# An mLSTM and two feed-forward layers on one core: the first layer's products in two row halves of the array

## The chip, the cores and the metric

The kernel runs on one core of a Trainium2 chip. The time is that of one execution on the device, in microseconds (us); the lower the better. Five engines work side by side, each through its own queue in order: PE (the matrix array, with its weight loads shown as PEld), DVE, ACT, POOL, and SP, which here only issues DMAs. An engine waits for another one, or for a DMA, at a semaphore.

## The reference

The inputs are q, k, v and an output gate of shape 2 x 8 x 768 x 40 (batch, head, position, head dimension), an input and a forget gate per position, and the weights of two feed-forward layers. All is float32.

```python
for t in range(S):                                # 768 positions
    m_new  = maximum(f[t] + m, i[t])
    f_stab, i_stab, m = exp(f[t] + m - m_new), exp(i[t] - m_new), m_new
    C = f_stab * C + i_stab * outer(v[t], k[t])   # 40 x 40 per head
    n = f_stab * n + i_stab * k[t]
    y[t] = sigmoid(o[t]) * (C @ q[t]) / maximum(abs(n . q[t]), 1)
x  = y as 1536 tokens x 320
xn = x / rms(x) * rms_g
x  = (silu(xn @ w_gate) * (xn @ w_val)) @ w_out   # first layer,  320 -> 1536 -> 320
h  = x @ w_in                                     # second layer, 320 -> 2048 -> 320
out = (maximum(h, 0) + alpha * minimum(h, 0)) @ w_out2
```

## The kernel before

**Stages.** The 768 positions are cut into six chunks of 128, and a chunk of one batch is a unit: units 0 to 11, of 128 tokens each. `attend` works out a unit: scores `sc` (L450), the part from the state `pv.../b` (L473), the weighted sum `pv` (L505), the new state `stp` (L529), then gate, division and scaling on ACT, DVE and POOL, and a transpose `trxn` (L627) that writes the unit's columns of `xh` and `xl`. The first layer takes groups m = 0, 1, 2 of 512 tokens (four units each). The second layer does the same with t2 = 0, 1, 2; its inputs go through a scratch tensor in memory and are transposed in 64-row halves (L657).

**Products in two parts.** Each float32 operand is split into a high part (a copy on ACT, fp32r) and a low part (what is left of it, from DVE or POOL). A product is high x high, high x low and low x high.

**First layer.** `moe1_in` (from L841) makes, for 128 hidden columns j of 512 tokens, two sums in a PSUM bank each: g from the gate's weights and v from the value's. `gemm_in` (L812) contracts over 320 rows in slabs of 128, 128 and 64. The third slab of the input stands twice, in rows 0 to 63 and again in rows 64 to 127, and the third slab of the weights has the high part of the gate's in the upper half and its low part in the lower one (for the value's the other way round), so that one matmul of 128 rows gives high and low together. That makes 8 matmuls of 512 columns for g and then 8 for v. After them come tanh (ACT, L856), silu (DVE, L859), the product with v (DVE, L862), the high part (ACT, L832) and the low part (DVE or POOL, L835). There are 36 such units of work: 12 for each m. For m = 0 the first four hold two j of 256 tokens each (32 matmuls of 256 columns), since only two units of tokens are there yet; the other 32 are wide (16 matmuls of 512 columns). `moe1_out` (L871) multiplies each result into four sums `acc` of 128 tokens, with three matmuls of 320 columns each (L826).

**Second layer.** `moe2_in` (from L933) has been working with 64 rows at a time: two sums h in two banks, and two matmuls side by side, one in rows 0 to 63 and one in rows 64 to 127 (L915). In phase 0 the upper rows write the first bank and the lower rows the second, 16 matmuls; in phase 1 the other way round, 14 matmuls. Between the phases stands `again` (L920): an ACT copy of one column of the input onto itself, which waits for phase 0 and on which phase 1 waits, so that no two halves write to a bank at once. `moe2_out` does the same with pairs of its four sums `accm` (L992, two runs of six matmuls, `again`, and two more runs with the banks changed).

**Order.** `plan` only notes steps, with the engine, a cost and the keys they read and write. `emit` (L79) then issues them in the order of the table `ORDER` (L1128), a list of step numbers; a trailing g puts a step on POOL that may run on DVE or POOL, and `*n` issues n idle matmuls on PE (`hot`, L1122; each shows as two in the profile). Each engine takes its steps in that order and waits where an input or one of the eight PSUM banks is not free.

**Names in the weights' preparation.** Weights come as raw words in blocks (`raw166w` and so on, from L695) and are decoded on ACT (L709, L715, L734), DVE (L719, L724) and DVE or POOL (L730, L738) before a product can use them.

## Time and profile before

| | us |
|---|---|
| median of three runs | 491.33 |
| their lowest and highest | 485.49, 492.27 |
| the profiled execution's own time | 490.37 |
| its span, first to last instruction | 488.6 |
| PE busy in the span | 463.8 (95%) |
| DVE, ACT, POOL busy | 321.6, 214.0, 154.3 |

Busy time counts the instructions of an engine from start to end, overlaps once. What lies between the span and the execution's own time is 490.37 - 488.6 = 1.8 us. The mean granted clock of the array over the span is 0.955 of the full 2.4 GHz; in a slice it is either near 1.00 or near 0.50 (1.2 GHz), or a mix of both.

### The profile page before, as it was taken

To read this page: it belongs to the slowest core of one execution; us is meant where nothing else is said; L and a number is where in the kernel's file an instruction comes from. 1 tells how busy PE (TensorE), PEld (TensorE's weight loads), DVE (VectorE), ACT (ScalarE), POOL (GpSimd) and SP (SyncE) were. 2 spreads that over 40 slices of the span, in tenths; PEclk is the share of its full clock that TensorE was granted. 3 is DMA by queue.
4 is the path that set the end of the run, shared out by engine and by line. 5 is a ranking of instruction groups with operands and counts; after the bars stand their busy time and mean duration, and the time that the engine had idled before them with its cause. 6 is when DMAs were issued, how large, how long until landed. Compare 5 with 4: busy or idle time off the path is not lost. (4 is left out here: it accounts for less than half of the span.)

```text
span 488.6 us, 9677 instructions
## 1 busy us (share of the span) xinstructions
PE 463.8 (95%) x3836; PEld 412.4 (84%) x3836; DVE 321.6 (66%) x592; ACT 214.0 (44%) x513; POOL 154.3 (32%) x156
## 2 busy tenths in 40 slices
PE   6988799989989999999998999999999999999996
PEld 5978798878869898888886888899989899888986
DVE  4669969889885554555487476598576475555354
ACT  3465674695543622533455534454523232222222
POOL 1242555687433203404156322221431101111310
PEclk9557799999999999999998999999999999999999
DMA  5657465455550311250134343063001010010001
GB/s 182 214 185 236 130 214 149 186 175 144 185 171 34 111 46 57 71 186 7 34 119 139 102 120 110 31 219 118 20 1 31 15 44 1 2 52 4 2 1 55
DMA packets 19149, 47.68 MB, mean 98 GB/s; under 512 B 2448, under 2 KB 8736, under 8 KB 19104
## 3 DMA queue, kind: packets, MB, share of 16 engines
q1 hardware_dynamic: 19104, 47.07, 30.2%
q8 instruction: 30, 0.49, 0.4%
q14 instruction: 15, 0.12, 0.1%
HBM read 40.07 MB, written 4.37 MB: 91 GB/s over the span
## 5 line engine op out<-in xcount | busy, mean ns | idle before, releaser
L962 DVE TENSOR_SCALAR tm<-hm,al_sb 128x512 f32<-128x512 f32 x48 | 35.3, 746 | 38.3 <-PE hm L915 27.0
L835 POOL TENSOR_TENSOR glm<-tm,ghm 128x512 fp32r<-128x512 f32 x17 | 21.9, 1293 | 110.2 <-ACT ghm L832 94.1
L832 ACT ACTIVATE ghm<-tm 128x512 fp32r<-128x512 f32 x48 | 29.8, 625 | 31.8 <-PE accm L992 16.7
L856 ACT ACTIVATE t<-g 128x512 f32<-128x512 f32 x36 | 21.3, 591 | 45.4 <-PE g L820 25.0
L835 DVE TENSOR_TENSOR glm<-tm,ghm 128x512 fp32r<-128x512 f32 x31 | 22.7, 737 | 27.2 <-ACT ghm L832 25.0
L859 DVE SCALAR_TENSOR_TENSOR t<-t,g 128x512 f32<-128x512 f32 x36 | 24.5, 682 | 24.4 <-ACT t L856 24.2
L835 POOL TENSOR_TENSOR gl<-t,gh 128x512 fp32r<-128x512 f32 x21 | 28.3, 1353 | 33.4 <-ACT gh L832 33.4
L832 ACT ACTIVATE gh<-t 128x512 fp32r<-128x512 f32 x36 | 22.4, 628 | 32.6 <-PE acc L826 16.5
L968 DVE SCALAR_TENSOR_TENSOR tm<-hm,tm 128x512 f32<-128x512 f32 x48 | 32.3, 686 | 0.8
L862 DVE SCALAR_TENSOR_TENSOR t<-t,v 128x512 f32<-128x512 f32 x36 | 24.4, 682 | 12.4 <-PE v L820 11.3
L505 PEld LDWEIGHTS pv<-vko,w 128*128 128x128 f32 x192 | 27.5, 220 | 4.6 <-DVE hn L482 3.0
L922 ACT ACTIVATE ghm<-ghm 128x1 fp32r<-128x1 f32 x48 | 9.6, 201 | 49.5 <-PE accm L992 49.3
L505 PE MATMUL pv<-vko,w 128*128 128x41 f32 x192 | 27.5, 303 | 3.6 <-DVE hn L482 2.3
L363 ACT ACTIVATE w<-w,col 128x128 f32<-128x128 f32 x80 | 26.5, 389 | 1.1 <-DVE col L297 0.8
L450 PE MATMUL sc<-r 40*128 40x128 f32 x192 | 18.5, 333 | 2.7 <-DVE xl L637 2.7
L450 PEld LDWEIGHTS sc<-r 40*128 40x128 f32 x192 | 15.6, 231 | 5.4 <-DVE xl L637 3.0
L574 POOL TENSOR_TENSOR vko<-vko,rd 128x320 f32<-128x320 f32 x7 | 6.9, 991 | 41.6 <-DVE rd L564 35.3
L454 DVE TENSOR_TENSOR w<-sc,w 128x512 f32<-128x512 f32 x24 | 16.0, 682 | 4.0 <-PE sc L450 3.1
L355 POOL TENSOR_SCALAR_AFFINE_SELECT w<-w 128x512 f32<-128x512 f32 x20 | 15.9, 812 | 8.0 <-ACT dec L370 7.9
L922 ACT ACTIVATE x2h<-x2h 128x1 fp32r<-128x1 f32 x24 | 4.8, 198 | 28.1 <-PE hm L915 28.1
L992 PE MATMUL accm<-o20h,ghm 64*128 64x320 f32 x96 | 16.8, 315 | 0.0
L992 PE MATMUL accm<-o20l,ghm 64*128 64x320 f32 x96 | 16.4, 306 | 0.0
(590 smaller groups left out, 1579.7 us busy)
## 6 DMA issues: line engine op xcount, KB each, us to landing
vko<-in_vko SPq DMA_DIRECT2D x12, 484.5 KB
w<-a_scr SPq DMA_DIRECT2D x10, 512.0 KB
r<-in_qk SPq DMA_DIRECT2D x24, 160.0 KB
y_scr<-y SPq DMA_DIRECT2D x12, 192.0 KB
x<-y_scr SPq DMA_DIRECT2D x12, 192.0 KB
out<-y SPq DMA_DIRECT2D x12, 160.0 KB
raw210w<-in_wo SPq DMA_DIRECT2D x1, 640.0 KB
raw218w<-in_wo SPq DMA_DIRECT2D x1, 640.0 KB
```

Of the source, the lines that this page charges most:

```text
L363: nc.scalar.activation(out=T[w][:, h], in_=T[w][:, h], func=AF.Exp, bias=T[f"col{c}"][:, g:g + 1])
L450: nc.tensor.matmul(T[f"sc{u}_{s}"][:, i], lhsT=q[:, 1, i], rhs=q[:, 0, i], start=True, stop=True)
L454: nc.vector.tensor_tensor(out=p, in0=T[f"sc{u}_{s}"], in1=p, op=ALU.mult)
L505: nc.tensor.matmul(ps[:, i, 0:V1], lhsT=T[w][:, h], rhs=v[:, h], start=True, stop=True)
L832: nc.scalar.activation(out=new(gh, "gh", [128, n], F32R), in_=T[t], func=AF.Copy)
L835: on[e].tensor_tensor(out=new(gl, "gl", [128, n], F32R), in0=T[t], in1=T[gh].bitcast(F32), op=ALU.subtract)
L856: nc.scalar.activation(out=new(t, "t", [128, 512]), in_=T[g], func=AF.Tanh, scale=0.5)
L859: nc.vector.scalar_tensor_tensor(out=T[t], in0=T[t], scalar=1.0, in1=T[g], op0=ALU.add, op1=ALU.mult)
L862: nc.vector.scalar_tensor_tensor(out=T[t], in0=T[t], scalar=0.5, in1=T[v], op0=ALU.mult, op1=ALU.mult)
L962: nc.vector.tensor_scalar(out=new(t, "t", [128, 512]), in0=T[ps], scalar1=0.0, scalar2=al_sb[:, j:j + 1], op0=ALU.min, op1=ALU.mult,)
L968: nc.vector.scalar_tensor_tensor(out=T[t], in0=T[ps], scalar=0.0, in1=T[t], op0=ALU.max, op1=ALU.add)
L992: nc.tensor.matmul(T[accs[a]][:, 0:DM], lhsT=g[HALF[s], a * 128:a * 128 + 128], rhs=w[HALF[s], j % 4], start=begin and k == 0, stop=end an ...
```

## The change

The first layer's products work with 64 rows at a time as well.

- `gemm_in` now serves both layers. For the first layer the two sums are g and v. In the first step (`swap` 0) the upper rows write g and the lower rows v, 16 matmuls; in the second step (`swap` 1) the upper rows write v and the lower rows g, 14 matmuls. The low x low product of the third slab, which the 128-row form made along with the others, is no longer made. Both sums end with the second step.
- `again` stands between the two steps. The narrow units have three steps (the second holds the end of the first j and the start of the second) and two `again`.
- `gemm_out` and the new `out_pair` serve both layers too. A pair of sums takes a step of six matmuls (per j), an `again` on a column of the result's high part, and a step of six with the banks changed. Which of the pair begins changes from one call to the next.
- `emit` leaves out an idle matmul where no bank would be free for it, and idle matmuls take a bank of their own each time.
- The order table is written anew, for 1986 steps in place of 1874: 108 of the new steps are `again` on ACT (40 between the steps of g and v, 68 in the pairs of sums) and 4 are the third steps of the narrow units. The tokens for idle matmuls add up to 9 in place of 23.

In the old table PE's first steps are: 5 + 1 + 1 + 1 idle matmuls around `ab1_1`, `ab0_0`, `ab0_1`, then scores of unit 0, the gates of chunk 1 (`gc1`, L289), `ab1_0`, `pv` of unit 0, its state, the scores and `pv` of unit 1, its state, `trxn0`, scores of units 2 and 3, `trxn1`, then g of the first layer's first unit. In the new table they are: the four `ab` with two idle matmuls between, the scores of units 0 and 1, `pv` of unit 0, `gc1`, `pv` of unit 1, the state of unit 0, scores of unit 2, `trxn0`, scores of unit 3, `trxn1`, the state of unit 1, then the first step of the first layer. ACT's first steps are, in the old table, the two copies of `sp` (L283), the first exponent (L396) and then the decoding of `raw166w` (L709); in the new one the decoding of `raw166w` stands first, and that of `raw174w` (L715, L709) before the first exponent. SP's first loads are, in the old table, gates, three blocks of r (q and k), `raw166w`, rg, gates of chunk 1, vko of unit 0, `raw174w`; in the new one gates, `raw166w`, rg, vko of unit 0, one block of r, `raw174w`, another block of r, gates of chunk 1, two more of r. From the scores of chunk 2 on the two tables place about as many DVE steps ahead of each of PE's steps (151 and 150 ahead of the gates of chunk 3, 237 and 237 ahead of those of chunk 4).

```diff
-        after, done, sums = {}, set(), []
+        done, sums, held = set(), [], set()
         for token in table.split():
             if token[0] == "*":
                 live = [x for x in sums if any(j not in done and self.steps[j][0] == "P" for j in self.users[x])]
+                held = {x for x in held if not done.issuperset(self.users[x])}
                 for _ in range(int(token[1:])):
-                    self.idle(live[-1] if live else None)
+                    if live or len(held) < self.slots["ps"]:
+                        self.idle(live[-1] if live else None)
                 continue
             i = int(token.rstrip("g"))
             eng, fn, deps, take, order = (self.steps[i][k] for k in (0, 2, 3, 4, 6))
@@ -90,6 +92,7 @@
             fn(*([("G" if token[-1] == "g" else "V")] if eng == "VG" else []))
             done.add(i)
             sums += [name for _, name, _ in take if name.startswith("acc")]
+            held.update(name for tag, name, _ in take if tag == "ps")
...
+    HALF = [slice(0, 64), slice(64, 128)]
+
+    def gemm_in(pss, W, cs, xh, xl, swap, back, first, last):
+
         wh, wl = W
-        sl = slice(c0, c0 + 128)
-        ops = []
-        for k in range(2):
-            ops += [(wh[:, k, sl], xh[:, k]), (wh[:, k, sl], xl[:, k]), (wl[:, k, sl], xh[:, k])]
-        ops += [(wh[:, 2, sl], xh[:, 2]), (wh[:, 2, sl], xl[:, 2])]
-        for i, (a, x) in enumerate(ops):
-            nc.tensor.matmul(ps, lhsT=a, rhs=x, start=(i == 0), stop=(i == len(ops) - 1))
-
-    def gemm_out(a, gh, gl, W, j, nj, i):
+        lists = []
+        for s in range(2):
+            rows, q = HALF[s], s ^ swap
+            sl = slice(cs[q], cs[q] + 128)
+            ops = [(wh[rows, 2, sl], xh[rows, 2])] if swap else []
+            for k in range(2):
+                ops += [(wh[rows, k, sl], xh[rows, k]), (wh[rows, k, sl], xl[rows, k]), (wl[rows, k, sl], xh[rows, k])]
+            if not swap:
+                ops += [(wh[rows, 2, sl], xl[rows, 2]), (wh[rows, 2, sl], xh[rows, 2])]
+            lists.append([(pss[q], *o) for o in (ops[::-1] if back else ops)])
+        n = len(lists[0])
+        for i, ops in enumerate(zip(*lists)):
+            for ps, w, x in ops:
+                nc.tensor.matmul(ps, lhsT=w, rhs=x, start=first and i == 0, stop=last and i == n - 1)
+
+    def gemm_out(accs, gs, cs, W, j, begin, end):
+
         wh, wl = W
-        sl = slice(i * 128, (i + 1) * 128)
-        for k, (g, w) in enumerate(((gh, wh), (gh, wl), (gl, wh))):
-            nc.tensor.matmul(
-                a[:, 0:DM], lhsT=g[:, sl], rhs=w[:, j % 4], start=(j == 0 and k == 0), stop=(j == nj - 1 and k == 2)
-            )
+        gh, gl = gs
+        for k, (g, w) in enumerate(((gh, wh), (gl, wh), (gh, wl))):
+            for s in range(2):
+                nc.tensor.matmul(
+                    T[accs[s]][:, 0:DM], lhsT=g[HALF[s], cs[s]:cs[s] + 128], rhs=w[HALF[s], j % 4],
+                    start=begin and k == 0, stop=end and k == 2
+                )
+
+    def again(ap, key):
+
+        plan("A", 60, lambda: nc.scalar.activation(out=ap(), in_=ap().bitcast(F32), func=AF.Copy), w=key)
+
+    turned_to = {}
+
+    def out_pair(accs, todo, wk, wt, begin, end):
+
+        o = turned_to.get(accs[0], 0)
+        turned_to[accs[0]] = 1 - o
+
+        def step(o, nm, cs, j, key, begin, end):
+            both, cols = [accs[o], accs[1 - o]], [cs[o], cs[1 - o]]
+
+            def f():
+                if begin:
+                    for a in accs:
+                        new(a, "ps", [128, 512])
+                gemm_out(both, (T[f"gh{nm}"], T[f"gl{nm}"]), cols, wt(j), j, begin, end)
+            plan("P", mm(3, 320), f, w=" ".join(accs), r=f"gh{nm} gl{nm} {wk(j)}" + (f" gh{nm}/{key}" if key else ""),
+                 take=[("ps", a) for a in accs] if begin else ())
+        key = f"t{accs[0][-1]}"
+        for x, (nm, cs, j) in enumerate(todo):
+            step(o, nm, cs, j, key if x == len(todo) - 1 else "", begin and x == 0, False)
+        nm, cs, j = todo[-1]
+        again(lambda nm=nm, c=cs[1 - o]: T[f"gh{nm}"][:, c:c + 1], f"gh{nm}/{key}")
+
+        def rest_of():
+            for x, (nm, cs, j) in enumerate(todo[::-1]):
+                step(1 - o, nm, cs, j, key if x == 0 else "", False, end and x == len(todo) - 1)
+        return rest_of
...
-        def prod(ps, c0):
-            if c0 == 0:
+        def prod(*parts):
+            if parts[0][2]:
                 new(g, "ps", [128, 512])
                 new(v, "ps", [128, 512])
-            for i in range(512 // n):
-                gemm_in(T[ps][:, n * i:n * i + n], win("w1", j // 2), c0 + 128 * (j % 2 + i),
-                        T[xh][:, :, t0:t0 + n], T[xl][:, :, t0:t0 + n])
+            for i, swap, first, last in parts:
+                c = 128 * (j % 2 + i)
+                gemm_in([T[ps][:, n * i:n * i + n] for ps in (g, v)], win("w1", j // 2), (c, 256 + c),
+                        T[xh][:, :, t0:t0 + n], T[xl][:, :, t0:t0 + n], swap, i, first, last)
...
-        for ps, c0 in ((g, 0), (v, 256)):
-            plan("P", mm(4096 // n, n), lambda ps=ps, c0=c0: prod(ps, c0), w=ps, r=wk,
-                 take=[] if c0 else [("ps", g), ("ps", v)])
+        steps = [[(0, 0, True, False)], [(0, 1, False, True)]]
+        if n == 256:
+            steps[1].append((1, 1, True, False))
+            steps.append([(1, 0, False, True)])
+        for x, todo in enumerate(steps):
+            plan("P", mm(sum(8 - p[1] for p in todo), n), lambda todo=todo: prod(*todo), w=f"{g} {v}", r=f"{wk} {xh}/t{t0}",
+                 take=[("ps", g), ("ps", v)] if x == 0 else ())
+            if x < len(steps) - 1:
+                again(lambda: T[xh][:, 2, t0:t0 + 1], f"{xh}/t{t0}")
...
     def moe1_out(nm, m, t0, n, j0):
-        gh, gl = f"gh{nm}", f"gl{nm}"
-        for i in range(4):
-            j, tok = j0 + 128 * i // n, t0 + 128 * i % n
-            u = 4 * m + tok // 128
-            acc = f"acc{u // 2}_{u % 2}"
-
-            def f(acc=acc, j=j, i=i):
-                if j == 0:
-                    new(acc, "ps", [128, 512])
-                gemm_out(T[acc], T[gh], T[gl], wout("o1", j // 4), j, NJ1, i)
-            plan("P", mm(3, 320), f, w=acc, r=f"{gh} {gl} {wkeys('o1', j // 4)}", take=[("ps", acc)] if j == 0 else ())
-            if j == NJ1 - 1:
-                moe1_end(u, acc)
+        names = [f"acc{u // 2}_{u % 2}" for u in range(4 * m + t0 // 128, 4 * m + (t0 + n) // 128)]
+        later = []
+        for p in range(n // 256):
+            pair = names[2 * p:2 * p + 2]
+            todo = [(nm, (256 * p + n * x, 256 * p + n * x + 128), j0 + x) for x in range(512 // n)]
+            later.append(out_pair(pair, todo, lambda j: wkeys("o1", j // 4), lambda j: wout("o1", j // 4),
+                                  j0 == 0, j0 == NJ1 - 1))
+        for f in later:
+            f()
+        if j0 == NJ1 - 1:
+            for i, acc in enumerate(names):
+                moe1_end(4 * m + i, acc)
...
-            lists = [
-                gemm_half(T[hs[x]], win("w2", i), 128 * b + 256 * x, T[xh], T[xl], s, x == s)
-                for s, x in ((0, phase), (1, 1 - phase))
-            ]
-            for ops in zip(*lists):
-                for f in ops:
-                    f()
+            gemm_in([T[h] for h in hs], win("w2", i), (128 * b, 128 * b + 256), T[xh], T[xl], phase, 0, phase == 0, phase == 1)
...
+        later = []
+        for q in range(2):
+            todo = [(f"m{t2}_{4 * i + 2 * x + b}", (256 * q, 256 * q + 128), 4 * i + 2 * x + b) for x in range(2)]
+            later.append(out_pair(accs[2 * q:2 * q + 2], todo, lambda j: wkeys("o2", i), lambda j: wout("o2", i),
+                                  p == 0, p == NJ2 // 2 - 1))
+        for f in later:
+            f()
...
-    hot = new("hot", "ps", [128, 512])
+    hot = []
 
     def idle(name):
 
-        ps = T[name][:, 384:512] if name else hot[:, 0:128]
+        if not name:
+            hot.append(new(f"hot{len(hot)}", "ps", [128, 512]))
+        ps = T[name][:, 384:512] if name else hot[-1][:, 0:128]
         nc.tensor.matmul(ps, lhsT=ident, rhs=ident, start=not name, stop=not name)
...
 ORDER = """
-0 7 1 8 *5 18 9 13 26 *1 10 11 *1 12 14 19 15 166 77 16 2 *1 17 31 4 6 76 21 78 79 22 20 167 3 80 23 81 174 82 27 35 83
...
+0 7 8 166 13g 9 4 20 1 10 11 18 14 174 167 15 12 26 168 17 77 76 176 16 27 2 169 175 31 23 *1 78 177 170 *1 21 19 22 24
+88 28 182 82 79 29 80 25 81 35 36 171g 89 83 56 84 40 30 38 32 37 178 39 194 33 57 44 179 183 58 6 172 61 100 41 42 180
```

## Rows read from the trace of the kernel before

**Rows 1.** Windows by stage: length, busy us (x instructions) per engine, granted clock, DMA share, GB/s.
```profile
0.00:57.50 57.50, 46.67 (x335) 42.90 (x336) 41.13 (x100) 31.02 (x76) 18.96 (x30) 0.72 0.60 192
57.50:140.00 82.50, 78.26 (x571) 68.98 (x571) 71.99 (x132) 49.86 (x116) 51.18 (x45) 0.97 0.55 175
140.00:230.00 90.00, 87.11 (x595) 76.70 (x595) 50.63 (x113) 35.95 (x91) 23.78 (x32) 0.98 0.24 81
230.00:304.00 74.00, 71.78 (x383) 62.06 (x382) 48.90 (x76) 36.73 (x71) 27.74 (x23) 0.98 0.34 103
304.00:488.60 184.60, 179.99 (x1959) 161.74 (x1957) 108.93 (x172) 60.45 (x164) 32.66 (x28) 1.00 0.12 40
```

**Rows 2.** Chain of waits (start us, us, what), the first layer's end, second layer's begin.
```profile
278.09 1.84 PE g L820 x8
279.93 0.43 PE acc L826 x3
280.36 1.84 PE v L820 x8
...
304.37 2.04 PE hm L915 x16
306.40 1.51 PE acc L826 x9
```

**Rows 3.** The same chain in the second layer.
```profile
380.39 1.86 PE hm L915 x16
382.26 0.43 PE accm L992 x6
382.69 1.81 PE hm L915 x14
...
391.25 1.84 PE hm L915 x16
393.09 4.39 PE accm L992 x60
397.49 1.61 PE hm L915 x14
```

**Rows 4.** Timeline of PE, the 256-column matmuls: first, second and last of one v.
```profile
46.62 0.28 PE L820 MATMUL v<-xl,w10h 128*128 128x256 f32 x1
46.74 0.28 PE L820 MATMUL v<-xh,w10l 128*128 128x256 f32 x1
...
48.29 0.28 PE L820 MATMUL v<-xl,w10h 128*128 128x256 f32 x1
```

**Rows 5.** Costliest groups: `again` in the second layer (busy us, mean ns; idle before, releaser).
```profile
L922 ACT ACTIVATE ghm<-ghm 128x1 fp32r<-128x1 f32 x48 | 9.6, 201 | 49.5 <-PE accm L992 49.3
```

**Rows 6.** Windows 356 to 476 us of one line each: L915, L992, L657, then ACT's L922.
```profile
356.00:476.00 120.00, 64.05 (x508) 47.05 (x510) 1.00 0.05 16
...
356.00:476.00 120.00, 65.38 (x790) 60.47 (x790) 1.00 0.05 16
...
356.00:476.00 120.00, 1.51 (x24) 1.43 (x24) 1.00 0.05 16
...
356.00:476.00 120.00, 9.85 (x51) 1.00 0.05 16
```

**Rows 7.** Timeline of PE in the first stage, with idle time before and its releaser.
```profile
12.51 0.28 PE L289 MATMUL gc<-ident,gate 16*128 16x16 f32 x1 [2.75 <-DVE gate L273]
15.56 3.48 PE L505 MATMUL pv<-vko,w 128*128 128x41 f32 x16
25.00 3.48 PE L505 MATMUL pv<-vko,w 128*128 128x41 f32 x16
41.59 0.56 PE L820 MATMUL g<-xh,w10h 128*128 128x256 f32 x1
```

**Rows 8.** Timeline of ACT in the first stage.
```profile
7.81 0.60 ACT L396 ACTIVATE w<-ab 128x512 f32<-128x512 f32 x1 [2.48 <-PE ab L389]
14.03 0.68 ACT L715 ACTIVATE lwraw174w<-raw174w 128x512 int32<-128x512 uint32 x1 [3.22 <-DMA raw174w<-in_wgv]
```

**Rows 9.** Chain of waits around 263 us.
```profile
262.73 0.61 DVE t L862
263.34 0.04 issue
263.38 5.51 PE g L820 x16
```

**Rows 10.** Waits of PE (total us, times, longest), two of them in the later stages.
```profile
PE g L820 <- DVE t L862: 2.2, 1, 2.2
...
PE accm L992 <- DVE glm L835: 0.6, 1, 0.6
```

More of the change, by code (lines that the diff above doesn't have):

```diff
@@ L900, in moe1_end @@
         plan("S", dma(196000), lambda: nc.sync.dma_start(out=y_scr[u], in_=T[y]), w=f"scry{u}", r=y)
-    HALF = [slice(0, 64), slice(64, 128)]
-    def gemm_half(ps, W, c0, xh, xl, s, own):
-        wh, wl = W
-        sl, rows = slice(c0, c0 + 128), HALF[s]
-        ops = []
-        for k in range(2):
-            ops += [(wh[rows, k, sl], xh[rows, k]), (wh[rows, k, sl], xl[rows, k]), (wl[rows, k, sl], xh[rows, k])]
-        if own:
-            ops.append((wh[rows, 2, sl], xl[rows, 2]))
-        ops.insert(len(ops) if own else 0, (wh[rows, 2, sl], xh[rows, 2]))
-        return [
-            lambda a=a, x=x, i=i: nc.tensor.matmul(
-                ps, lhsT=a, rhs=x, start=own and i == 0, stop=not own and i == len(ops) - 1
-            ) for i, (a, x) in enumerate(ops)
-        ]
-    def again(ap, key):
-        plan("A", 60, lambda: nc.scalar.activation(out=ap(), in_=ap().bitcast(F32), func=AF.Copy), w=key)
     def x2_unit(u):
@@ L975, in moe2_out @@
         accs = [f"accm{t2}_{r}" for r in range(4)]
-        for r in range(4):
-            lower = (r + 2 * (p % 2)) % 4
-            both = (lower, (lower + 2) % 4)
-            for x in (range(2) if r < 2 else (1, 0)):
-                j = 4 * i + 2 * x + b
-                nm = f"m{t2}_{j}"
-                begin = p == 0 and x == 0 and r < 2
-                def f(both=both, j=j, nm=nm, begin=begin, end=p == NJ2 // 2 - 1 and x == 0 and r > 1):
-                    if begin:
-                        for a in both:
-                            new(accs[a], "ps", [128, 512])
-                    wh, wl = wout("o2", i)
-                    gh, gl = T["gh" + nm], T["gl" + nm]
-                    for k, (g, w) in enumerate(((gh, wh), (gl, wh), (gh, wl))):
-                        for s, a in enumerate(both):
-                            nc.tensor.matmul(
-                                T[accs[a]][:, 0:DM], lhsT=g[HALF[s], a * 128:a * 128 + 128], rhs=w[HALF[s], j % 4],
-                                start=begin and k == 0, stop=end and k == 2
-                            )
-                plan("P", mm(3, 320), f, w=" ".join(accs[a] for a in both),
-                     r=f"gh{nm} gl{nm} {wkeys('o2', i)}" + (f" gh{nm}/{r % 2}" if x else ""),
-                     take=[("ps", accs[a]) for a in both] if begin else ())
-            if r < 2:
-                again(lambda nm=f"ghm{t2}_{4 * i + 2 + b}", c=128 * both[1]: T[nm][:, c:c + 1], f"ghm{t2}_{4 * i + 2 + b}/{r}")
+        later = []
[5 more added lines that the diff above has]
+            f()
         if p < NJ2 // 2 - 1:
```

142 lines of the change are left out of this document (73 added, 69 removed), and 3 rows, old and new, of the table ORDER.

## The prediction

> **What bounds the kernel now.** I read the windows by stage first, since a share over the whole span mixes stages with different limits. They show PE busy for 46.7 of 57.5 us at the start, for 78.3 of 82.5 us next, and for 96.8% or more in the three later stages, at a granted clock of 0.97 and above [rows 1]. So from 57.5 us on the time is PE's: work taken from PE there shortens the run, and a hole on PE lengthens it. DVE is the nearest rival, at 72.0 of 82.5 us (87%) in the second stage, and at 56 to 66% later. The first stage is another matter: PE runs there at a mean clock of 0.72, with idle matmuls among its work, and what counts is how soon the attention of chunks 0 and 1 hands inputs to the first layer, whose first matmul starts at 41.6 us [rows 1, 7]. Next I read the chain of waits for what each piece costs when PE is fed. It gives both layers side by side, so the second layer, which already works in row halves, prices the new form of the first. The list of PE's waits then says that PE's profiled holes are few: the longest one after 57.5 us is 2.2 us, in front of a g [rows 10].
>
> **The change, term by term.** The sum is made against the profiled execution's 490.37 us, which is 0.96 us below the median of 491.33.
>
> *The products of g and v.* A wide unit takes 8 + 8 matmuls of 128 rows now, 1.84 + 1.84 = 3.68 us [rows 2]. In row halves the second layer does 16 in 1.84 to 1.86 us and 14 in 1.61 us [rows 3], so the pair of half matmuls costs the same 0.23 us as one of 128 rows, and the unit costs 1.85 + 1.61 = 3.46 us. What is saved is one of 16 passes, the low x low product of the third slab. That is 0.22 us for each of 32 wide units, 7.0 us. About 8 of these units lie between 57.5 and 140 us and 24 after it, so nearly all of this is on PE's path.
>
> *The narrow units.* Four units of 32 matmuls with 256 columns: 14 intervals take 48.29 - 46.62 = 1.67 us, 0.119 us each [rows 4], or 3.82 us a unit. In halves they are 30 pairs. No row shows a pair of 256 columns. From below it is the same 0.119 us, which gives 3.58 us; from above it is the pair of 320 columns, 60 matmuls in 4.39 us, 0.146 us a pair [rows 3], which gives 4.39 us. I take the lower end, because at 320 columns the pair costs what the full matmul costs (three in 0.43 us, 0.143 us each [rows 2]): 4 x 0.24 = 1.0 us saved. The upper end would be 2.3 us lost.
>
> *The four sums.* Six half matmuls of 320 columns take 0.43 us [rows 3], and three full ones 0.43 us [rows 2]. Nothing is gained or lost in 36 x 4 such runs.
>
> *108 `again`.* Each is an ACT instruction of 0.20 us [rows 5] that waits for PE, and the step after it waits for ACT. Its work, 21.7 us, lies on an engine that is busy for 60%, 40% and 50% of the stages concerned [rows 1], and adds some 9% to it; the cover is ACT's own idle time, and without it each would push tanh and the high parts back by 0.2 us. The price that reaches PE is the hole between the two steps. With one run of sums as the only cover (0.43 us), the second step took 1.81 us instead of 1.61: a hole of 0.20 us [rows 3]. The mean price comes from a calm window of 120 us: 508 matmuls of h at 3.46 / 30 = 0.115 us are 58.6 us, 790 of sums at 4.39 / 60 = 0.073 us are 57.8 us, the transposes 1.5 us [rows 3, 6]; 2.1 us are left for 51 `again`, 0.04 us each. In the new table I counted what stands on PE between the two steps of each unit: 8 of the 40 places have at most one run of sums (about 0.43 us), 10 have two, 22 have more. Of the 68 places in the pairs of sums 4 have less than 0.7 us of cover. So 12 places at 0.20 us and 96 at 0.04: 2.4 + 3.8 = 6.2 us lost. The ends are 108 x 0.04 = 4.3 and 108 x 0.20 = 21.6 us.
>
> Behind a waiting `again` stand, on ACT, the tanh and high parts of other units, and for them wait DVE, POOL and the next run of sums. That is the same pattern as in the second layer, where `again` waited 49.3 us for sums without PE starving [rows 5, 10].
>
> *Later ends of g.* tanh could start when g was done, 1.84 us before v; now g and v end together. The chain of tanh, silu, product and parts starts later, and both banks are held longer. PE has the sums of earlier units to do meanwhile, so I cost it at nothing; if that cover is gone, PE waits for a bank as at 263 us: 2.2 us of waiting for the DVE product of an older unit, and then a g that took 5.51 us for 16 matmuls instead of 3.68, as its clock had fallen to half: 4.0 us in all [rows 9, 10].
>
> *Changes of form.* Going from full rows to halves, the first 16 matmuls of h took 2.04 us instead of 1.84, and the way back 9 matmuls of sums 1.51 instead of 1.30 [rows 2]. That is 0.2 us a change. The first layer joins the second in form, but the attention's full-row steps now stand among halves: I count 59 changes in the new order against 55. 0.8 us lost.
>
> *The start.* PE no longer waits 2.75 us for chunk 1's gates ahead of the first `pv`, and `pv` of unit 1 follows that of unit 0, where it started at 25.00 us although the first had ended by 19.0 [rows 7]: the gain is at most about 25.0 - 19.3 = 5.7 us. Against it, ACT now decodes `raw174w` ahead of the first exponent. This exponent ran at 7.81 us, and `raw174w` was there at 14.03 us [rows 8]; the SP queue has somewhat less ahead of it now, but `pv` of unit 0 could be as much as 1.5 us later than its 15.56. The 14 idle matmuls that go ran in idle time and are costed at nothing, their cover being PE's waits in this stage; where they kept the clock up, their loss is inside the upper end. Between -5.7 and +1.5 I take the middle, -2.0, as from the scores of chunk 2 on DVE has as much to do before each of PE's steps as it had.
>
> *Weights, scratch transfers, the second layer.* Same instructions and DMAs; only which pair of sums goes together changes. Nothing.
>
> Sum: -7.0 - 1.0 + 6.2 + 0.8 - 2.0 = -3.0 us, from 490.4 to about 487.4 us: **487 us**, 0.9% below the median shown. The saving in work and the holes nearly cancel; the sign hangs on the start.
>
> **The rivals.**
>
> *Holes (slower).* The place is between the two steps of every unit and pair of the first layer. In the second layer ACT is busy for 33% of the time, here for 40 to 60% [rows 1], and an `again` that is due behind a 0.63 us activation comes late. If each of the 108 costs the 0.20 us of the barely covered one [rows 3], the sum is -8.0 + 21.6 + 0.8 - 2.0 = +12.4: 502.8 us. It decides from (501.2 - 490.4 + 9.2) / 108 = 0.185 us each. For it: ACT's load. Against it: 22 of 40 and 64 of 68 places have a longer cover than the row has. The Trainium skill, TensorEngine Tiling (Array Packing), section Restrictions and Gotchas, says that row tiles must not reach one PSUM bank at the same time, that software has to keep them apart, and that row tiling raises the pressure on PSUM. It speaks against the change and names no price; the hole of 0.20 us agrees with it [rows 3], and by the rule alone, with no cover anywhere, the time would be this rival's.
>
> *Banks (slower).* Four new holes like that at 263 us, at 4.0 us each [rows 9, 10], put on the forecast: 503.4 us. In the first half attention wants two banks for scores and two for `pv` beside four sums. Against it: between 140 and 304 us the old table left PE idle for only 2.9 + 2.2 us, with the banks shared in the same way [rows 1].
>
> *Start and order (faster).* The start gives all of its 5.7 us, and the new table has no hole like that at 263 us: -8.0 + 6.2 + 0.8 - 5.7 - 4.0 = -10.7: 479.7 us, 2.4% below the median. For it: the removed wait is plain in the rows. Against it: DVE at 87% in the second stage [rows 1] can eat what the start brings.
>
> *The halves don't overlap.* 30 matmuls at 0.23 us would cost 6.9 us a unit, over 100 us more in all. The 16 in 1.84 us exclude it, as good as [rows 3].
>
> **How the numbers follow.** A measurement here can tell about 2% from no change, 481.5 to 501.2 us. Forecast 0.54, faster rival 0.25, holes 0.13, banks 0.07, no overlap 0.01. So faster 0.25, same 0.54, slower 0.21. The forecast's own range is 482 to 494: holes from 4.3 us up, narrow units up to 3.3 us worse, the start from -5.7 to +1.5. The range of 8 in 10 takes in the faster rival with some of the spread of a new order below it and reaches to the slower rivals' centres: 473 to 503; left out are some 0.07 below and 0.11 above.
>
> **What would show it.** Wide units at about 3.46 us in two pieces of 16 and 14, with the sums' runs of six at 0.43 us, would confirm the work saved. Second steps of 14 over 1.8 us in most units would show the holes. `again` ended late behind ACT's longer instructions, and waits of PE for DVE's L859 or L862, would show ACT's queue and the banks. The first g's start against 41.6 us shows the start. I am wrong if PE's busy work falls by much else than 8 us, if its idle time grows past 20 us after 57.5 us, or if the clock stays at half for longer than now.

## The result and the profile after

**3.0% faster in one series and 2.1% in a second: 475.12 us (472.88 to 481.54) against 490.54, ratio 0.970 [0.965, 0.976]; with the same kernel again 478.88 (474.44 to 480.83) against 489.62, ratio 0.979 [0.974, 0.984].** The profiled execution took 472.88 us, its span is 471.1 us. Medians here and below are over all executions; the ratios leave out those more than 1.5% above the fastest of their kernel, which are the 481.54 us here, three of the six with the old start (483.04 to 488.89 us) and three of the six with the longer `again` (486.89, 487.80 and 562.06 us), and one of the kernel before (493.77 us).

The granted clock differs from one execution to the next, and this has to be taken out first. Most executions of one kernel are shorter when their mean granted clock is higher: before took 485.05 and 485.27 us at 0.972 and 489.62 to 490.96 at 0.953 to 0.955; after took 472.88 and 473.80 at 0.971 and 478.33 at 0.953. At equal clock and on one chip, in the second series, the change gives 11.3 to 11.5 us at 0.968 (485.70 and 485.93 against 474.44), 11.3 to 12.0 at 0.953 (489.62 and 490.36 against 478.33) and 10.0 at 0.957 to 0.958 (489.40 against 479.42): 10 to 12 us. The match is a rough one between two kernels, since the mean counts the start as full clock whatever the array did there (shown below with the idle matmuls). The two profiles, 17.5 us apart, met different clocks (0.955 and 0.971), so their first stages can't be compared to the microsecond.

I cut both kernels at the same events: the first g, the first wide unit, the first g of m = 1, that of m = 2, the first hm, and the end. The windows of the kernel before (columns as in rows 1):

```profile
0.00:41.59 41.59, 34.04 (x216) 31.30 (x217) 26.08 (x69) 19.38 (x47) 11.52 (x22) 0.64 0.59 188
41.59:83.31 41.72, 37.92 (x355) 35.62 (x355) 36.48 (x79) 28.03 (x69) 20.85 (x21) 0.91 0.60 192
83.31:151.20 67.89, 62.15 (x395) 52.83 (x394) 60.14 (x105) 39.20 (x88) 41.31 (x36) 0.97 0.50 158
151.20:237.83 86.63, 85.76 (x592) 76.47 (x590) 45.57 (x102) 35.02 (x86) 23.34 (x32) 1.00 0.22 74
237.83:304.30 66.47, 64.25 (x333) 54.55 (x332) 44.39 (x68) 31.94 (x61) 24.93 (x20) 0.97 0.37 111
304.30:488.60 184.30, 179.69 (x1957) 161.63 (x1956) 108.93 (x172) 60.45 (x164) 32.36 (x28) 1.00 0.12 40
```

The same stages of the changed kernel:

```profile
0.00:36.82 36.82, 25.77 (x187) 22.65 (x187) 25.20 (x68) 20.75 (x49) 10.67 (x21) 0.78 0.79 234
36.82:79.17 42.35, 38.83 (x486) 35.96 (x486) 39.14 (x82) 29.73 (x83) 24.47 (x28) 0.91 0.57 183
79.17:147.31 68.14, 62.32 (x639) 54.18 (x639) 57.80 (x107) 41.88 (x109) 30.53 (x30) 0.97 0.53 165
147.31:229.67 82.36, 82.27 (x884) 73.73 (x882) 44.34 (x98) 38.93 (x121) 21.66 (x29) 1.00 0.21 69
229.67:289.89 60.22, 60.09 (x621) 56.57 (x619) 38.11 (x60) 36.10 (x91) 29.01 (x23) 1.00 0.35 103
289.89:471.10 181.21, 176.97 (x1997) 168.92 (x1993) 107.42 (x169) 62.75 (x174) 44.26 (x36) 1.00 0.15 46
```

The differences are -4.8, +0.6, +0.3, -4.3, -6.3 and -3.1 us. The last three stages, 337.4 against 323.8 us, are at full clock but for the hole at 263 us in the kernel before, and they repeat: in the second profile of the same kernel they took 82.33, 60.28 and 181.20 us. In stages 4 and 5 PE now has 0.09 and 0.13 us of idle time where it had 0.87 and 2.22. The list of PE's waits has no entry from 147.3 us on; the ones of [rows 10] are gone. A hole of 0.2 us doesn't show in that list; it shows as a longer first pair of matmuls, as below.

The chain of waits in stage 5, to be read beside [rows 2, 3] (start us, us, what):

```profile
244.16 0.43 PE acc L841 x6
244.59 0.42 PE v L833
...
246.40 0.43 PE acc L841 x6
246.83 0.23 PE g L833
...
248.67 0.88 PE acc L841 x12
...
250.66 0.21 PE v L833
...
252.28 1.75 PE acc L841 x24
```

A first step of 16 takes 248.67 - 246.83 = 1.84 us, a second one of 14 behind a longer cover 252.28 - 250.66 = 1.62, and a run of six sums 0.43: the pieces that the prediction took from the second layer. Behind only 0.43 us of cover the second step's first pair shows 0.42 us instead of 0.23, a hole of 0.19. On the timeline of PE, of the 24 units of stages 4 and 5, the five with one run of sums as cover have holes of 0.13 to 0.21 us, and the eight with two runs (0.88 us) have none over 0.05 us (0.23 us for the first pair at 187.59 us, for instance). On the timeline of PE, two of the narrow units' g matmuls (their v matmuls lie beside them) are 0.12 us apart, the lower of the two bounds:

```profile
53.38 0.28 PE L833 MATMUL g<-xl,w11h 64*128 64x256 f32 x1
53.50 0.28 PE L833 MATMUL g<-xh,w11l 64*128 64x256 f32 x1
```

The start, on the timeline of PE and then on that of ACT, beside [rows 7, 8]:

```profile
7.35 0.77 PE L384 MATMUL ab<-tri,idr 128*128 128x512 f32 x1 [7.35 <-DVE idr L216]
...
16.80 1.95 PE L508 MATMUL pv<-vko,w 128*128 128x41 f32 x16
...
18.90 1.09 PE L508 MATMUL pv<-vko,w 128*128 128x41 f32 x8
...
36.82 0.55 PE L833 MATMUL g<-xh,w10h 64*128 64x256 f32 x1 [1.40 <-ACT lwraw210w L718]
```

```profile
11.51 0.66 ACT L718 ACTIVATE lwraw174w<-raw174w 128x512 int32<-128x512 uint32 x1 [4.59 <-DMA raw174w<-in_wgv]
```

`raw174w` is there at 11.51 us rather than at 14.03. The first `pv` begins 1.24 us later than before, inside the 1.5 us that the prediction allowed, but the next one begins 2.1 us after it, at 18.90 us, where it was 9.4 us. The first g starts 4.8 us earlier.

The new instructions on ACT, from the page's costliest groups:

```profile
L848 ACT ACTIVATE gh<-gh 128x1 fp32r<-128x1 f32 x68 | 13.4, 197 | 27.5 <-PE acc L841 27.4
L848 ACT ACTIVATE xh<-xh 128x1 fp32r<-128x1 f32 x40 | 8.0, 200 | 32.0 <-PE v L833 30.8
```

All 108 are there, at 0.20 us each, and ACT waits for PE in front of them, not the other way round: the list of PE's waits of the whole run has `xh` of L848 with 0.9 us in all.

### The profile page after: what moved, and what is told of

It reads as the page before. It is cut to its first block, busy times and chain, and to the rows that moved or that the text cites. A ratio compares the mean times of both kernels' runs of the same rounds, so it can differ in the third digit from the quotient of the medians.

```text
span 471.1 us, 11760 instructions
## 1 busy us (share of the span) xinstructions
PE 446.2 (95%) x4798; PEld 412.0 (87%) x4798; DVE 312.0 (66%) x582; ACT 230.1 (49%) x621; POOL 160.6 (34%) x166
## 4 chain that ended last, share of the span: by engine, by line
PE 74%; DVE 13%; issue 7%; ACT 3%; POOL 2%; DMA 0%; DVEq 0%; POOLq 0%; ACTq 0%
PE accm L841 17%; PE hm L833 16%; PE g L833 10%; PE v L833 10%; PE acc L841 9%; PE pv L508 4%; PE sc L453 2%; PE pv L476 2%; PE trxn L630 1%; DVE o12l L741 1%; DVE lwraw262w L722 1%; DVE t L908 1%; DVE w L457 1%; PE stp L532 1%; DVE t L911 1%
## 5 line engine op out<-in xcount | busy, mean ns | idle before, releaser
L883 POOL TENSOR_TENSOR glm<-tm,ghm 128x512 fp32r<-128x512 f32 x26 | 34.5, 1328 | 113.7 <-ACT ghm L880 96.0
L908 DVE SCALAR_TENSOR_TENSOR t<-t,g 128x512 f32<-128x512 f32 x36 | 24.5, 682 | 38.3 <-ACT t L905 35.6
L883 POOL TENSOR_TENSOR gl<-t,gh 128x512 fp32r<-128x512 f32 x18 | 24.8, 1380 | 27.6 <-ACT gh L880 27.6
L848 ACT ACTIVATE ghm<-ghm 128x1 fp32r<-128x1 f32 x48 | 9.1, 199 | 44.4 <-PE accm L841 44.2
L883 DVE TENSOR_TENSOR glm<-tm,ghm 128x512 fp32r<-128x512 f32 x22 | 15.6, 708 | 21.0 <-ACT ghm L880 21.0
L508 PEld LDWEIGHTS pv<-vko,w 128*128 128x128 f32 x192 | 23.4, 197 | 4.9 <-DVE hn L485 2.8
L848 ACT ACTIVATE gh<-gh 128x1 fp32r<-128x1 f32 x68 | 13.4, 197 | 27.5 <-PE acc L841 27.4
L911 DVE SCALAR_TENSOR_TENSOR t<-t,v 128x512 f32<-128x512 f32 x36 | 24.6, 683 | 2.0
L848 ACT ACTIVATE xh<-xh 128x1 fp32r<-128x1 f32 x40 | 8.0, 200 | 32.0 <-PE v L833 30.8
L848 ACT ACTIVATE x2h<-x2h 128x1 fp32r<-128x1 f32 x24 | 4.8, 202 | 33.0 <-PE hm L833 33.0
L841 PE MATMUL acc<-o11h,gh 64*128 64x320 f32 x96 | 19.1, 319 | 0.0
L841 PE MATMUL accm<-o23h,ghm 64*128 64x320 f32 x96 | 18.8, 311 | 0.0
L841 PE MATMUL accm<-o23h,glm 64*128 64x320 f32 x96 | 18.6, 308 | 0.1
L841 PE MATMUL accm<-o23l,ghm 64*128 64x320 f32 x96 | 18.5, 306 | 0.0
L841 PE MATMUL acc<-o11h,gl 64*128 64x320 f32 x96 | 18.4, 306 | 0.0
```

Of the source, the lines that this page charges most:

```text
L508: nc.tensor.matmul(ps[:, i, 0:V1], lhsT=T[w][:, h], rhs=v[:, h], start=True, stop=True)
L841: nc.tensor.matmul(T[accs[s]][:, 0:DM], lhsT=g[HALF[s], cs[s]:cs[s] + 128], rhs=w[HALF[s], j % 4], start=begin and k == 0, stop=end and k == 2
L848: plan("A", 60, lambda: nc.scalar.activation(out=ap(), in_=ap().bitcast(F32), func=AF.Copy), w=key)
L883: on[e].tensor_tensor(out=new(gl, "gl", [128, n], F32R), in0=T[t], in1=T[gh].bitcast(F32), op=ALU.subtract)
L908: nc.vector.scalar_tensor_tensor(out=T[t], in0=T[t], scalar=1.0, in1=T[g], op0=ALU.add, op1=ALU.mult)
L911: nc.vector.scalar_tensor_tensor(out=T[t], in0=T[t], scalar=0.5, in1=T[v], op0=ALU.mult, op1=ALU.mult)
```

## The experiments

All but the first are edits of the changed kernel, and where no other kernel is named they are compared with its stages above.

**The same kernel again.** The edit is a comment; what it is for is the spread of times and of stages.

> The changed kernel once more, unaltered, on the chip and beside the kernels of this call, as their yardstick: 473 to 477 us, with stages of about 36.8, 42, 68, 82.4, 60.2 and 181 us; the second and third vary with the granted clock.

Measured: 478.88 us, ratio 0.979 [0.974, 0.984], 2 us above the expected range, on the same chip as three of the experiments below. The last three stages agree with those of the first profile within 0.1 us; the first three took 148.9 us, not 147.3, with the clock at 0.84 in stage 2. Sub-microsecond readings are good in the last three stages and worthless in the first three.

**The new order with the old form.** g, v and the four sums in 128 rows, `again` of the first layer left out; the order table stays.

```diff
-                gemm_in([T[ps][:, n * i:n * i + n] for ps in (g, v)], ..., swap, i, first, last)
+                gemm_full(T[(g, v)[swap]][:, n * i:n * i + n], win("w1", j // 2), c + 256 * swap, ...)
...
-                again(lambda: T[xh][:, 2, t0:t0 + 1], f"{xh}/t{t0}")
+                plan("A", 60, lambda: None, w=f"{xh}/t{t0}")
```

> The new order with the old form: both of the first layer's products in 128 rows again (g in the place of the first step, v in that of the second, each run of sums full), its 108 `again` issue nothing; the second layer and every other step stand as in the new table. Theory 1, form and order share the gain: the order alone gives the earlier start (4.8 us) and the missing hole at 263 us (4.0 us) and some of the rest, the form gives its one pass of 16 where PE is the bound, 24 units x 0.22 = 5.3 us: 480 to 483 us. Rival, all is order: 474 to 477 us. Rival, all is form: 488 to 491 us.

Measured: 482.82 us, ratio 0.989 [0.985, 0.994]. Its last three stages:

```profile
151.25:237.95 86.70, 86.64 (x574) 75.44 (x572) 44.14 (x98) 33.56 (x85) 22.16 (x30) 0.98 0.20 65
237.95:301.22 63.27, 63.27 (x336) 53.99 (x335) 38.73 (x63) 32.45 (x60) 27.42 (x23) 1.00 0.34 105
301.22:485.70 184.48, 179.28 (x1957) 166.90 (x1956) 104.88 (x167) 60.97 (x165) 43.56 (x36) 1.00 0.14 43
```

Stage 5 is 3.2 us shorter than before with the old form still in it, and PE is busy in all of it: the hole at 263 us went with the order, not with the halves. (There is one profile of the old order; of the profiles of the new one, only that with no cover has a wait over 0.5 us in the list from stage 4 on.) The halves give the rest, 4.3, 3.1 and 3.3 us of these three stages; in stage 4 some 0.02 x 86.7 = 1.7 us of that is clock. In the executions at a clock of 0.968, before took 485.7 to 486.3 us, this kernel 480.4 to 482.4, and the changed one 474.4: order and start gave some 3 to 6 us, the form 6 to 8. These executions are from different chips, and the ratio's interval alone gives 3 to 7 us for order and start.

**The dropped product put back.** One pair more in each second step of the first layer: 16 + 16 matmuls for a wide unit.

```diff
             ops = [(wh[rows, 2, sl], xh[rows, 2])] if swap else []
+            if swap and more:
+                ops.append((wh[rows, 2, sl], xl[rows, 2]))
```

> The changed kernel with the low x low product of the third slab put back into the second step of each unit (16 + 16 half matmuls in place of 16 + 14), all else as it is. It prices the work saved. If PE bounds throughout after the first g: 32 x 0.23 + 4 x 2 x 0.12 = 8.3 us more, 483 us. If only the stages after 147 us are bound by PE, 24 x 0.23 = 5.5 us more, 480 to 481 us. Rival, the saved pass lies in slack: 475 to 476 us.

Measured: 483.23 us, ratio 0.988 [0.985, 0.992].

```profile
154.32:239.12 84.80, 84.80 (x908) 76.24 (x906) 43.72 (x98) 39.02 (x121) 21.84 (x29) 1.00 0.21 67
239.12:301.82 62.70, 62.70 (x647) 55.46 (x645) 38.95 (x61) 36.26 (x91) 28.51 (x23) 1.00 0.34 102
```

Stages 4 and 5 are 2.44 and 2.48 us longer, 0.20 to 0.21 us for each of their 12 units, where the prediction had 0.22. Over the whole kernel, at clocks of 0.968 and 0.971, it took 480.5 and 480.7 us against 474.4 and 472.9, and at 0.957 it took 484.6 to 484.8 against 479.4: 5 to 8 us for 7.0 + 1.0 predicted. This term was right, and on PE's path.

**The old start.** The first 168 steps in the old table's order, with its idle matmuls, then the new table.

```diff
-0 7 8 166 13g 9 4 20 1 10 11 18 14 174 167 15 12 26 168 17 77 76 ...
+0 7 1 8 *5 18 9 13 26 *1 10 11 *1 12 14 19 15 166 77 16 2 *1 17 ...
```

> The changed kernel with the old table's first 168 steps and their idle matmuls, up to the first g, and the new table's order for all that is left. Theory, the start is carried to the end: first g at 41 to 42 us again, 479 to 481 us. Rival, DVE bounds the second stage and eats the start: 475 to 476 us, with the scores of chunk 4 at about 157 us as in the changed kernel.

Measured: 480.85 us, ratio 0.977 [0.973, 0.981].

```profile
0.00:40.86 40.86, 35.67 (x216) 32.12 (x216) 25.74 (x69) 21.14 (x51) 11.53 (x22) 0.66 0.61 191
```

The first g is 4.0 us later, and the next three stages are as long as in the changed kernel's second profile (43.81, 68.12 and 82.40 against 44.03, 68.16 and 82.33), so in this trace the delay is carried through. In the times it is smaller, 474.93 us at a clock of 0.971 against 472.88 and 473.80 (1 to 2 us), 477.80 at 0.968 against 474.44 (3.4 us), and 478.66 at 0.961 against 479.54 (0.9 us less); the intervals of the ratios overlap. The start is worth anything from nothing to some 4 us; the experiment doesn't fix it closer.

**A longer `again`.** 256 columns in place of one in all 108 `again` of the first layer, 0.41 us in place of 0.20.

```diff
-        again(lambda nm=nm, c=cs[1 - o]: T[f"gh{nm}"][:, c:c + 1], f"gh{nm}/{key}")
+        wide = 1 if accs[0].startswith("accm") else 256
+        again(lambda nm=nm, c=min(cs) if wide > 1 else cs[1 - o]: T[f"gh{nm}"][:, c:c + wide], f"gh{nm}/{key}")
...
-                again(lambda: T[xh][:, 2, t0:t0 + 1], f"{xh}/t{t0}")
+                again(lambda: T[xh][:, 2, t0:t0 + 256], f"{xh}/t{t0}")
```

> The changed kernel with each `again` of the first layer copying 256 columns in place of one (0.2 us becomes about 0.4 us on ACT, 108 times), everything else as it is. Theory, the holes are covered by other steps on PE: 0 to 3 us more, 475 to 478 us. Rival, PE waits for each round trip: 108 x 0.19 = 20 us more, 495 us.

Measured: 485.30 us, ratio 0.982 [0.977, 0.987]. Its executions at a clock of 0.971 took 477.27 and 478.08 us, 3.5 to 5.2 above the changed kernel's at that clock: above the theory's 0 to 3, and far from the rival's 20. In its profiled execution, of 487.80 us, the clock was lower in stages 2 and 3 (0.74 and 0.93), so I read stages 4 and 5 only.

```profile
158.72:241.96 83.24, 82.75 (x884) 74.69 (x882) 43.86 (x98) 46.42 (x120) 21.86 (x29) 1.00 0.21 68
241.96:304.84 62.88, 61.82 (x623) 53.53 (x620) 38.91 (x61) 42.52 (x92) 28.89 (x23) 1.00 0.35 103
```

ACT gets 7.5 and 6.4 us more to do. Stage 4 with its 36 `again` grows by 0.88 us, 0.02 each, and stage 5 with 31 by 2.66, 0.09 each, of the 0.21 us added to each. Cover hides most of a longer `again` too, and less of it in stage 5.

**Halves for g and v alone, and for the sums alone.** The other part keeps 128 rows; all else is the changed kernel. With the sums alone, the low x low product stays and the 40 `again` of g and v go; with g and v alone, the 68 of the sums go.

The edit for g and v alone, cut short (the second layer's sums, `accm`, keep `gemm_out`):

```diff
-                gemm_out(both, (T[f"gh{nm}"], T[f"gl{nm}"]), cols, wt(j), j, begin, end)
+                nc.tensor.matmul(T[both[0]][:, 0:DM], lhsT=g[:, cols[0]:cols[0] + 128], rhs=w[:, j % 4], ...)
```

> The changed kernel with g and v in row halves, but the first layer's four sums in full rows (their 68 `again` issue nothing), in the same order. Theory, a change between full rows and halves costs PE about 0.25 us (the old form in the new order lost 3.3 us in the last stage for 13 changes): 162 changes stand in this order against 59, 103 x 0.25 = 26 us more where PE bounds, at least the 80 of the last three stages, 20 us: 493 to 500 us, no better than before the change. Rival, changes of form cost nothing and the saved pass stays: 473 to 476 us.

> The changed kernel with the four sums in row halves, but g and v in full rows, 8 + 8 matmuls (their 40 `again` issue nothing), in the same order. Theory: 150 changes of form against 59, 91 x 0.25 = 23 us, at least 70 x 0.25 = 17.5 us in the last three stages, and the saved pass is lost, 5 to 8 us: 496 to 505 us. Rival, changes of form cost nothing: 479 to 482 us.

Measured: g and v alone 490.27 us, ratio 1.006 [1.001, 1.010], a little under the theory's range; sums alone 497.78 us, ratio 1.019 [1.013, 1.024], inside it. The windows of the first, stages 4 to 6, and then two pieces of its chain of waits:

```profile
152.56:240.74 88.18, 88.11 (x742) 74.13 (x741) 44.17 (x98) 35.77 (x96) 22.27 (x30) 0.98 0.20 64
240.74:308.15 67.41, 67.41 (x502) 50.84 (x501) 38.31 (x61) 33.65 (x71) 27.70 (x23) 1.00 0.34 104
308.15:491.10 182.95, 178.95 (x1957) 167.01 (x1956) 106.73 (x169) 61.58 (x167) 43.94 (x36) 1.00 0.13 41
```

```profile
260.94 1.07 PE acc L872 x6
262.02 0.20 PE trx23a L660
```

The windows of the second:

```profile
153.49:245.30 91.81, 91.77 (x714) 74.13 (x712) 43.97 (x98) 36.98 (x108) 21.71 (x29) 0.98 0.19 62
245.30:314.70 69.40, 69.40 (x453) 52.83 (x452) 39.01 (x63) 34.19 (x79) 27.97 (x23) 1.00 0.31 101
```

In this one order the old form took 482.82 us, g and v alone 7.5 us more, the sums alone 15.0 us more, and both together 4 to 8 us less (478.88 and 475.12). These are medians from different chips, but the ratios, 0.989, 1.006, 1.019 and 0.979 or 0.970, have the same order. The order was made for both; what either half would take in an order of its own, with its products of one form put side by side, was not tried. PE is busy for all of these stages in both; it just takes longer. What differs is how often PE goes from matmuls of 128 rows to matmuls of 64 or back. Six sums in full rows behind halves take 1.07 us here, where six in the kernel before, among full rows, took 0.88 us: 0.19 for one change. I counted the changes between 128 rows and fewer (64, 40 or 16) along PE's matmuls in order of time, for stages 4, 5 and 6:

| kernel | changes in stages 4, 5, 6 | whole run |
|---|---|---|
| before | 10, 7, 4 | 45 |
| after | 14, 0, 0 | 51 |
| new order, old form | 18, 9, 12 | 73 |
| halves for g and v alone | 39, 41, 13 | 153 |
| halves for the sums alone | 45, 38, 0 | 143 |

Per change, against the kernel after: g and v alone 7.19 / 41 = 0.18 us in stage 5, 1.74 / 13 = 0.13 in stage 6, and in stage 4, less 1.8 us for the clock of 0.98, 4.0 / 25 = 0.16. Sums alone, less 2.5 us a stage for the product put back: (9.18 - 2.5) / 38 = 0.18 in stage 5, and with 1.8 us for the clock (9.45 - 2.5 - 1.8) / 31 = 0.17 in stage 4. The new order with the old form gives 3.27 / 12 = 0.27 in stage 6. So a change costs 0.13 to 0.27 us, about what [rows 2] said (0.2). The Trainium skill, TensorEngine Tiling (Array Packing), Key Properties, says that a change of the tiling mode drains the array, where a change of the tile alone doesn't; it gives no price. These stages agree.

**No cover.** In the order table each unit's first step of g and v is put right ahead of its `again` and the second step right behind it; in 37 of 40 places nothing stands between.

```diff
-... 778 791 779 718 980 958 780 ...
+... 778 779 780 718 980 ...
```

> The changed kernel with the cover between the steps of g and v taken away: each unit's first step is moved to stand right ahead of its `again` and the second right behind it, so that at 37 of 40 places PE has nothing else in between (26 of the 40 have two or fewer runs in the changed kernel). Same instructions. Theory, a hole is the round trip of about 0.6 us less the cover (0.2 us were left behind 0.43 us): 24 x 0.6 = 14 us more in the stages of m = 1 and 2, up to 24 us in all: 487 to 500 us, the gain of the change gone. Rival, the round trip is short or hidden otherwise: 474 to 480 us.

Measured: 516.98 us, ratio 1.058 [1.054, 1.063], 17 us above the theory's range. (The expectation counts 26 places with two or fewer runs, where the prediction's 8 and 10 make 18.) Its stages 4 and 5:

```profile
164.01:259.27 95.26, 89.74 (x884) 74.26 (x882) 43.56 (x98) 37.55 (x115) 21.64 (x29) 0.96 0.19 60
259.27:332.09 72.82, 65.61 (x616) 52.49 (x614) 37.65 (x61) 34.82 (x91) 28.25 (x23) 0.98 0.31 91
```

Its chain of waits around one hand-over, and then an entry of the list of PE's waits (total us, times, longest), for the whole run and for stage 4:

```profile
265.08 0.22 PE g L833
...
265.41 0.21 ACT xh L848
...
265.66 0.50 PE v L833
...
266.17 0.23 PE v L833
```

```profile
PE v L833 <- ACT xh L848: 13.2, 36, 1.7
...
PE v L833 <- ACT xh L848: 4.0, 12, 0.4
```

The stages grow by 12.9 and 12.6 us, 1.05 to 1.08 us a unit, and 40 places make 42 us, the difference of the two profiles' spans. In the chain 266.17 - 265.30 = 0.87 us lie between the last pair of the first step and the second pair of the second, where 0.23 would do: 0.64 us for the way from PE to ACT and back. The other units are like it: 23 of these 24 have a hole of about 0.6 us there, which makes some 14 of the 25.5 us, as the expectation had it. The rest is not ACT coming late at these places (the longest wait is 0.4 us in both stages; the 1.7 us lies ahead of them). It is lost clock (0.96 and 0.98, some 3.8 and 1.5 us) and other waits that came with the new order of steps (1.3 us for DVE's L908 and L911 in stage 4, 3.2 us for L883 and L908 in stage 5). So the holes are real, three times the 0.20 us that the prediction had as the upper price, five times with all that followed, and it is the order that hides them. The Trainium skill, TensorEngine Tiling (Array Packing), Restrictions and Gotchas, leaves it to software to keep row tiles off one bank; this run is the price, 0.6 us each, where nothing covers it.

**Idle matmuls.** PE waits 7.35 us at the start, and from 20 to 40 us the changed kernel's granted clock is 0.53 and then 0.50. Two edits: 12 idle matmuls ahead of the first step, and none in the whole table.

```diff
-0 7 8 166 13g 9 4 ...
+0 *12 7 8 166 13g 9 4 ...
```

```diff
-... 31 23 *1 78 177 170 *1 21 19 ...
+... 31 23 78 177 170 21 19 ...
```

> The changed kernel with 12 idle matmuls at the very start, where PE waits 7.35 us for the first input. Theory A, PE's half clock from 7.35 to 13.4 us delays the first scores and pv: the four ab steps take 1.0 us each as in the kernel before, pv of unit 0 starts 2 us sooner, 471 to 474 us. Theory B, the exponents on ACT behind the decoding of raw174w (11.5 us) and DVE's queue set the start of pv: first g at 36 to 37 us as now, 473 to 477 us.

> The changed kernel without its 9 idle matmuls in the first 52 us. They ran where PE waited. Theory A, they keep nothing warm: PE works at half clock from 24 to 41 us with them, so 473 to 479 us as before, perhaps 1 us sooner at the first g. Theory B, the clock of the second stage hangs on them: granted clock below 0.84 there and 480 to 486 us.

Measured: with 12 more 481.61 us, ratio 0.985 [0.981, 0.990]; with none 476.59 us (473.49 to 479.08), ratio 0.974 [0.970, 0.978]. Stage 1 with 12 more, and lines of PE's timeline in it:

```profile
0.00:38.06 38.06, 30.49 (x211) 27.48 (x211) 25.20 (x69) 20.59 (x49) 10.29 (x21) 0.71 0.75 226
```

```profile
8.08 0.43 PE L392 MATMUL ab<-sel,sp 128*128 128x512 f32 x1
...
13.86 2.02 PE L453 MATMUL sc<-r 40*128 40x128 f32 x30 [1.82 <-DMA r<-in_qk]
16.37 3.61 PE L508 MATMUL pv<-vko,w 128*128 128x41 f32 x16 [0.48 <-issue]
```

Products of the same form in the changed kernel, at 8.66 and at 14.25 us:

```profile
8.66 0.73 PE L392 MATMUL ab<-sel,sp 128*128 128x512 f32 x1
...
14.25 0.43 PE L392 MATMUL ab<-sel,sp 128*128 128x512 f32 x1
```

The idle matmuls did bring the array to full speed sooner: at 8.08 us the product takes 0.43 us, which it reaches in the changed kernel only behind 13.4 us. It doesn't help. The scores behind it wait 1.82 us for their load, `pv` begins only 0.4 us sooner, and it takes 3.61 us in place of 1.95, as the granted clock is 0.50 from 16 us on and not from 20.7. The first g is 1.2 us later, at 38.06 us. So both theories missed: A was right on the `ab` and wrong on `pv`, and the time is 4.6 us above B's range, against 478.88 us for the changed kernel on the same chip.

The mean clock misleads here. The rows give 1.00 for 7.35 to 13.40 us of the changed kernel, in which the product takes 0.73 us and not 0.43. The mean over a span counts that start as full, so the 0.78 of stage 1 without the idle matmuls and the 0.71 with them can't be compared, nor the 0.947 to 0.953 over all six executions with the changed kernel's 0.948 to 0.971. Without any idle matmuls the clock in stage 2 is 0.88, not below 0.84, and the times cover the same span as with them, as theory A had it. The nine that the new table has left do nothing that I can measure, and none of these kernels is better than the changed one.

## Why the prediction was right or wrong

The time, 475 us, lies inside the range, but the likeliest case, 487 us, is not what happened. What happened is the rival "start and order faster", 479.7 us: its 10.7 us below the kernel before stand against 10 to 12 measured at equal clock. That this sum came out is in part luck: it has the start at 5.7 us, more than the times show, and `again` at 6.2, also too much, and the two errors cancel. And one of the prediction's own signs of being wrong appeared: PE's busy work fell by 17.6 us (463.8 to 446.2), not by 8. Some 8.3 of that is in the first stage (34.0 to 25.8), where fewer idle matmuls run and the first `pv` takes 1.95 us and not 3.48; 10.4 us are in the last three.

- *PE bounds the later stages.* Right: whatever took work from PE there, or put it back, moved the stage by that much (the dropped product, 2.44 and 2.48 us).
- *Wide units, narrow units, sums: -8.0.* Right. The steps take 1.84 and 1.62 us, the sums 0.43 for six, the narrow pairs 0.12 us; putting the product back cost 5 to 8 us.
- *108 `again`: +6.2.* Mis-sized. In stage 5 of the changed kernel 360 half matmuls at 0.115 us, 233 to 237 of sums at 0.073 and 0.8 us of transposes are 59.2 to 59.6 of 60.22 us. Some 0.6 to 1.0 us are left for 31 `again`, 0.02 to 0.03 each: an estimate of 2 to 3 us for all 108. It is a small remainder of large numbers, as the prediction's 0.04 us was, but the places show the same: three of the twelve units in that stage have one run of sums as cover, with holes of 0.14 to 0.21 us, and those with two runs have none. So the rule "no more cover than 0.43 us costs 0.20" holds, and what was too high is the 0.04 us for the rest. With no cover a hole is 0.6 us, so the upper price was no upper bound; only the order kept it from mattering.
- *Changes of form: +0.8.* The price was right. The step that doesn't hold is "I count 59 changes in the new order against 55", which gives a change the same price wherever it stands. The trace has 51 against 45, and in stages 4 to 6, which PE bounds, 14 against 21, with none once the first layer works without attention: some 7 x 0.13 to 0.27 = 0.9 to 1.9 us gained. In the first three stages there are 37 against 24, and what those 13 more cost isn't shown, so the sign over the whole run stays open. The prices are also why, in this order, the halves of the change had to be made together.
- *Later ends of g: 0.* Right: from 147.3 us on PE waits for nothing on the list.
- *The start: -2.0 between -5.7 and +1.5.* The first g came 4.8 us earlier. The times don't settle what that is worth: from nothing to some 4 us.
- *The order in the bound stages: nothing.* The largest error: the forecast priced the new order at the start only and left the hole at 263 us in, with the loss of 4.0 us that I had worked out [rows 9, 10] counted in a rival alone. The old form in the new order has no such hole, and stage 5 is 3.2 us shorter by it. A table written anew keeps no particular accident of the old one.

For stages 4 and 5, at -10.5 us, the terms close to within a microsecond: -4.9 for the dropped product, -4.0 for the hole, -0.7 of other idle time, -0.4 to -0.8 for three changes of form less, -2.2 because 15 sums' worth of full matmuls (273 before; 515 halves after) now stand in stage 3, and some +1.3 for 67 `again`: -10.9 to -11.3. Stage 6, at -3.1, has four changes less (-0.5 to -1.1) and the wait of 0.6 us for `glm` [rows 10]; 1.4 to 2.0 us of it stay open. In stages 2 and 3 the saved work doesn't show as a shorter stretch; the sums that moved there (2.2 us), eight more changes of form (26 against 18) and the clock work against it, and I can't separate them. The new form in the old order was not tried.

## What to carry to other kernels

Before a form of matmul is changed in one place, count the changes of form in the stages that PE bounds, not in the whole run, and change neighbours together: in the new order either half alone was 7.5 or 15 us slower than the old form, and both together 4 to 8 us faster. A hand-over of banks between two halves left no hole over 0.05 us behind 0.88 us of independent work, 0.13 to 0.21 us behind 0.43 us, and 0.6 us with nothing between. When an order is written anew, price the holes of the old one as gone unless a resource makes them.

## What the runs showed of the hardware

The granted clock of the same kernel differs from one execution to the next, and in these runs it was worth more than several terms of the sum: after, 472.88 us at 0.971 to 480.83 at 0.950. In its two profiles all of it lies in the first three stages, in which attention still runs. It is no strict scale: executions of before with 0.993 took 488.85 and 488.79 us, and two with the old start at 0.982 took 483.04 and 488.89. Nor does it say how fast the array ran at the start: there the rows give 1.00 while a product took 0.73 us in place of 0.43. Idle matmuls ahead of the real work did bring full speed forward (0.43 us at 8.08 us), and the kernel was not faster for it, since the clock also fell sooner and the next load was not there yet.
